# A recurrent chain and a feed-forward layer on one core: four steps of the chain's slot moved, and one more pair of chunks inverted in blocks of 32

## The chip, the cores and the metric

The kernel runs on one core of one Trainium2 chip. A core has TensorE (matrix products and transposes into PSUM), VectorE, ScalarE, GpSimd and a sync engine (SP) that only issues DMAs and waits. Each engine runs its own instructions in order, and the engines meet through semaphores. The metric is the device time of one execution in microseconds; the median of several runs counts. Everything is fp32.

## The reference

For each of 4 batches and 8 heads a state of 40 x 40 is carried over 768 steps; its output, with heads side by side, is the token matrix of a feed-forward layer with a squared relu.

```python
for t in range(S):                                   # S = 768, B = 4, H = 8, D = 40
    y[:, :, t] = einsum('bhd,bhde->bhe', rt, state)
    Sa = einsum('bhde,bhe->bhd', state, at)
    state = state * wt[:, :, None, :] - einsum('bhd,bhe->bhde', Sa, bt)
    state = state + einsum('bhd,bhe->bhde', vt, kt)
x = y.transpose(0, 2, 1, 3).reshape(B * S, H * D)    # 3072 x 320
h = np.maximum(x @ w_in, 0.0)                        # 320 x 2048
out = h * h @ w_out                                  # 2048 x 320
```

## The kernel before

The 768 steps are cut into 6 chunks of 128, and the 4 batches are taken in turn, so that there are 24 chunks: chunk `i` is batch `i % 4`, and a chunk needs the state that chunk `i - 4` left. Inside a chunk the recurrence becomes matrix products: cumulative products of `w` (`decay`, forwards and backwards from the middle of the chunk) scale the inputs, a strictly triangular matrix `N` of products of `b` and `a` has to be inverted, and the rest is products with the state and the masked matrices `A`, `RV` and `RX`.

**Three kinds of work run side by side.**

- *Preparation* (`early`, wrapped by `prepare`): for a chunk some slots ahead, the transposes of `w`, `b`, `a`, the scans (L352, L353) and reciprocals (L357, L358), the products `ps_w<-decay,bT`, and the stores of the decays (`kept_e`) and of `N` (`kept_n`, and by rows `kept_q` or `kept_d`) to DRAM.
- *Inversion on GpSimd* (`take`, `solving`): chunks are grouped in units of 1, 1, 2, 2, 2, 2, 4, 4, 4 and 2. `take` fetches a unit's rows from DRAM into `half_n` (L420) once all its chunks are stored, `solving` runs one multiply and one subtract per step (L448, L450), and L453 stores the result to `kept_t`. The first `FINE` units are inverted in blocks of 32 steps, and their two blocks are then joined by small products on TensorE (`inverses`, second half; it needs the blocks' off-diagonal part, which `early` stores as `kept_m`). The other units are inverted in blocks of 64. The one unit in `AHEAD`, which is `(FINE,)`, is solved in two parts: 33 steps at once, and the rest only after the first part of the next unit's fetch has been issued, in the loop at the end of the kernel. GpSimd waits in order at each fetch for the rows' stores.
- *The chain and the feed-forward layer*: slot `i` runs the eleven pieces of `chain(i)`, and woven between them, for chunk `j = i + 1`: `turn_rv`, `make_rv` (`RV`), `turn_k`, `decay_state`, `turn_down`, `scale_kb`, `turn_state`, `make_a`, and the loading of its inverse (`inverses`, L464 for `T`, L473 for `N`). The layer's work (`Ffn`) is cut into quads (`thirds` and `whole`: the first product, then relu on ScalarE, L735), squares on VectorE (`square`, L742) and quarters (`make_quarter`: the second product and, every fourth time, the output's store).

**What sets the order.** Slots 0 to 3 (`woven`) interleave generators by counts. From slot 4 on `sorted_slot` writes the order out by hand, as a list of `step(...)` calls; after each, `tick` issues the stores that have come due (`later`, `store`; L108). Loads and stores share the sync engine's queue, which works in order; only GpSimd's fetches and result stores go through its own. The buffers concerned: `kept_here` holds the decays (`dec`) of two chunks, the rings of `k`, `b` and `v` two tiles each, the ring of `r` one. At the beginning of slot `i` the local function `loads` issues `k`, `dec` and `b` of chunk `i + 1`. `extra` (only in slot 4) adds quads of the layer, while the weights are still being converted (`rounding`).

Small copies: `turn_k` copies the last decay of the chunk to `ends` (L512), the chain copies its other end to `end` (L664), and `decay_state` multiplies the two (L533) and scales the state in two halves (L536).

Of the kernel before, what the change touches and what calls it, by code (L numbers as in the profile page):

```python
# [11 lines left out]
Alu = mybir.AluOpType  # L12
# [5 lines left out]
def kernel(  # L18
# [22 lines left out]
    nc = tc.nc  # L41
# [4 lines left out]
    C = 128  # L46
# [45 lines left out]
    def new(name, shape, bufs):  # L92
        return work.tile(shape, FP32, tag=name, name=name, bufs=bufs)
# [204 lines left out]
    sizes = [1, 1] + [2] * 4 + [4] * ((len(order) - 12) // 4) + [2]  # L298
    units = [(sum(sizes[:u]), n) for u, n in enumerate(sizes)]

    FINE = 4
    SMALL = units[FINE][0]
    kept_q = dram.tile([SMALL, H, 2, 2, Q, Q], FP32, tag="q", name="kept_q")
    kept_m = [dram.tile([2, Q, H, Q], FP32, tag=f"m{i}", name=f"kept_m{i}") for i in range(SMALL)]
# [120 lines left out]
    def solving(u, between={}, stop=None):  # L425

        first, nb = units[u]
        fine = u < FINE
        size = Q if fine else HC
        cols = classes(u)  # L430
        rows = 128 // cols
        part = part_of(u)
        words = size // cols * size
        at = u * Q * Q // 2 if fine else 0
        ts = solved[:, at:at + words]
        nc.gpsimd.memset(ts, 0.0)
        for col in range(cols):
            nc.gpsimd.memset(ts[col * rows:(col + 1) * rows, col::size + cols], -1.0)
        t3 = ts.rearrange("p (j t) -> p j t", t=size)
        for s in range(size - 1):  # L440
            if s in between:
                between[s]()
            if s == stop:
                yield
            n, m_ = s // cols + 1, size - 1 - s
            at = s * size + s + 1 if s < Q else Q * HC + (s - Q) * (Q + 1) + 1
            p_ = new("half_p", [128, 528], 1)[:, :n * m_].rearrange("p (j t) -> p j t", j=n)
            nc.gpsimd.tensor_tensor(p_, part[:, at:at + m_].unsqueeze(1).to_broadcast([128, n, m_]),  # L448
                                    t3[:, :n, s:s + 1].to_broadcast([128, n, m_]), Alu.mult)
            nc.gpsimd.tensor_tensor(t3[:, :n, s + 1:], t3[:, :n, s + 1:], p_, Alu.subtract)  # L450
        to = kept_t[u]
        to = to.rearrange("n b h f k j t -> (n b h f k) (j t)") if fine else to.rearrange("n b h f j t -> (n b h f) (j t)")
        nc.gpsimd.dma_start(out=to, in_=ts)  # L453
# [53 lines left out]
    def turn_k(i, g):  # L507
        kT, kT_ = turned("kvT", 1), turn(g["x"]["k"])
        down = g["dec"][:, DOWN]
        nc.vector.tensor_tensor(kT, kT_, down[:, :, 1:C + 1], Alu.mult)  # L510
        g["kT"], g["ends"] = kT, new("ends", [128, NP], 2)
        nc.vector.tensor_copy(g["ends"], down[:, :, 0])  # L512

    def make_a(i, g):
        g["A"] = masked("A", 2, g["kT"], g["aT"])
# [11 lines left out]
    def decay_state(i, g):  # L527
        bb, c = order[i]
        if c == 0:
            return  # L530
        st = states.tiles[bb]
        f_ = new("f", [128, NP], 1)
        nc.vector.tensor_tensor(f_, ended[bb], g["ends"], Alu.mult)  # L533
        for e in range(2):
            own_ = st[e * DP:(e + 1) * DP, :, e, :D]
            nc.vector.tensor_tensor(own_, own_, f_[e * DP:(e + 1) * DP].unsqueeze(2).to_broadcast([DP, NP, D]), Alu.mult)  # L536
# [32 lines left out]
    def rest(i, g):  # L569
        begin(i, g)  # L570
        yield
        yield
        turn_k(i, g)
        joining = inverses(i, g) if i else iter(())
        if soon(i):
            next(joining, None)
        yield
        make_a(i, g)
        yield
        turn_rv(i, g)  # L580
        yield
        decay_state(i, g)
        make_rv(i, g)
        if i and unit_of[i] < FINE:
            next(joining)
        yield
        turn_down(i, g)
        yield
        scale_kb(i, g)
        turn_state(i, g)  # L590
        yield
        yield from joining
        yield
# [6 lines left out]
    def chain(i, g):  # L600
# [54 lines left out]
        if c < NCH - 1:  # L655
            grown = psum(ps_c)[:, :NP * 2 * D].rearrange("p (q d) -> p q d", q=NP)
            for l_, r_ in ((k_, v_), (b_, xn)):
                for q in range(NP):
                    mm(grown[:, q].rearrange("p (e d) -> p e d", e=2), pair(l_, q), r_[:, 2 * q:2 * q + 2, :D], l_ is k_ and q == 0)
            for e in range(2):  # L660
                rows = slice(e * DP, (e + 1) * DP)
                nc.vector.tensor_tensor(st[rows, :, e, :D], grown[rows, :, e * D:(e + 1) * D], st[rows, :, e, :D], Alu.add)
            ended[bb] = new(f"end{bb}", [128, NP], 1)
            nc.vector.tensor_copy(ended[bb], g["up"][:, :, C])  # L664
        yield
        rx = masked("RX", 2, xT, rT)
        yield
# [237 lines left out]
    def fetch_next(i, *names):  # L905
        if i < len(order):
            loaded.setdefault(i, {}).update({nm: fetch(nm, {"k": k, "b": b, "r": r, "v": v}[nm], i) for nm in names})

    def sorted_slot(i, g, ch):
        j = i + 1  # L910
        more = j < len(order)
        n = ready.setdefault(j, {}) if more else None
        made = [prepare(m_, apart=True, steps=4 * at) for at, m_ in enumerate(ahead.get(i, ()))]
        one, two = (made + [iter(()), iter(())])[:2]
        joining = inverses(j, n) if more else iter(())
        early_join = more and soon(j)
        fine = more and unit_of[j] < FINE

        def step(*what):
            for w_ in what:  # L920
                w_()
            tick()

        of = lambda fn: (lambda: fn(j, n)) if more else (lambda: None)
        on = lambda gen: lambda: next(gen, None)
        begun = i > B

        def extra():
            if not begun:
                second.thirds()  # L930
                second.whole()

        halves = lambda: [next(rounded, None) for _ in range(2)] if not begun else None

        def loads():
            if more:
                fetch_next(j, "k")
                n["dec"] = kept_here[j % 2]
                nc.sync.dma_start(out=n["dec"][:USED], in_=kept_e[j])
                fetch_next(j, "b")  # L940

        loads()
        step(on(ch), halves)
        if more:
            begin(j, n)
        step(of(turn_rv), on(one), second.make_quarter, on(one), halves)
        step(on(ch), halves)
        if early_join:
            next(joining, None)
        fetch_next(j + 1, "r")  # L950
        step(second.make_quarter, halves)
        extra()
        step(on(ch))
        step(of(make_rv), second.thirds)
        step(on(ch), on(one), on(two), on(two))
        if fine:
            next(joining, None)
        step(second.whole, on(two))
        step(on(ch))
        step(on(one), of(turn_k))  # L960
        step(on(ch), of(decay_state), on(one), of(turn_down), of(scale_kb))
        step(on(ch), of(turn_state), second.square)
        if fine:
            next(joining, None)
        step(on(ch), of(make_a), second.thirds, on(one))
        fetch_next(j + 1, "v")
        step(second.whole, on(two), on(two))
        if not early_join:
            next(joining, None)
        step(on(ch), extra)  # L970
        step(on(ch))
        if more:
            later_chain = n["chain"] = chain(j, n)
            next(later_chain)
        run(ch)
        step(second.square, second.make_quarter)
        step(second.make_quarter, on(two))
        for gen in (one, two, joining):
            run(gen)

    for i in range(len(order)):
        tc.no_sync_barrier()
        g = ready.pop(i)
        ch = first_slot if i == 0 else g["chain"]
        done.update(ahead.get(i, ()))
        if i < B:
            woven(i, g, ch)
            n = ready[i + 1]
            n["chain"] = chain(i + 1, n)
            next(n["chain"])  # L990
            if i == B - 1:
                fetch_next(i + 2, "r", "v")
        else:
            sorted_slot(i, g, ch)
        while unit < len(units) and all(m_ in done for m_ in range(len(order)) if unit_of[m_] == unit):
            flush()
            if under_way:

                take(unit, own, slice(0, EARLIER))
                run(under_way.pop())  # L1000
                take(unit, own, slice(EARLIER, Q * (HC + Q)))
            else:
                take(unit, own)
            if unit in AHEAD:
                under_way.append(solving(unit, stop=Q + 1))
                next(under_way[0])
            else:
                solve(unit)
            unit += 1
# [32 lines left out]
```

## Time and profile before

| what | value |
|---|---|
| runs | 1097.03, 1095.37, 1087.47 us, median 1095.37 |
| profiled execution | 1094.95 us, span 1093.2 us |
| granted TensorE clock, mean | 0.87 |
| TensorE matmuls busy | 952.3 us (87% of the span) |
| TensorE weight loads busy | 785.3 us (72%) |
| GpSimd busy | 669.4 us (61%) |
| VectorE busy | 491.6 us (45%) |
| ScalarE busy | 284.4 us (26%) |
| DMA | 106.92 MB, mean 98 GB/s |
| chain that ended last, by engine | TensorE 66%, VectorE 12%, DMA 8% |

A line of a view names the source line, the engine, the operation and the tiles as `out<-in`; the number in brackets is how long the engine had stood idle before it and who released it. In the table by slices each digit is the busy share of one fortieth of the span (27.3 us) in tenths. The windows' rows give the stretch, its length, the time TensorE was busy and its instructions, the granted clock, the DMA engines' busy share and GB/s. A wait's row gives the waiting engine with its line, who released it, the total, how often and the longest. Matmul ends are modelled, so busy time on TensorE is not work at its peak. L87 is the helper of all plain products and L108 that of delayed stores, so the tiles tell which step a row belongs to.

### The profile page before, as it was taken

The page shows a single profiled execution, that of the slowest core. Times are in us where ns is not written, and L with a number is a line of the kernel's source. Part 1 is how long each engine was busy: PE and PEld are TensorE (multiplying, and loading weights), DVE is VectorE, ACT ScalarE, POOL GpSimd, SP SyncE. Part 2 cuts the span into 40 slices and gives each one's busy share as a digit, 9 for nine tenths or more (in the row PEclk, how much of TensorE's full clock was granted, in tenths as well). Part 3 has the DMA queues.
Part 4 walks back from the last instruction along what each step waited for, and adds up shares of the span by engine and source line. Part 5 has one row for each costly group of instructions (what it writes and reads, how often), then busy time and mean ns, then how long its engine had stood idle before and what let it go on. Part 6 is the DMA issues. An engine that isn't in the chain of part 4 may idle for free.

```text
span 1093.2 us, 19699 instructions
## 1 busy us (share of the span) xinstructions
PE 952.3 (87%) x7728; PEld 785.3 (72%) x7728; DVE 491.6 (45%) x908; ACT 284.4 (26%) x643; POOL 669.4 (61%) x1128
## 2 busy tenths in 40 slices
PE   6275765685899899999899999999999999999998
PEld 5264654674788787778677877878888887777776
DVE  5456683784554435537246345344323433231111
ACT  3133241332231322222312222212222222322111
POOL 4788544886885399993699976999768810000000
PEclk8666575566998898999988998989999999999999
DMA  8878969678144862654873655541644314230000
GB/s 109 145 141 165 174 168 177 147 150 138 43 82 108 143 118 58 98 98 117 142 125 58 100 132 110 95 85 26 136 90 84 65 37 92 47 63 7 13 13 12
DMA packets 261376, 106.92 MB, mean 98 GB/s; under 512 B 244100, under 2 KB 250372, under 8 KB 259620
## 3 DMA queue, kind: packets, MB, share of 16 engines
q1 hardware_dynamic: 256756, 86.65, 44.4%
q0 software_dynamic: 3440, 18.88, 7.5%
q8 instruction: 61, 1.00, 0.4%
q10 hardware_dynamic: 1088, 0.13, 0.1%
q14 instruction: 31, 0.25, 0.1%
HBM read 72.47 MB, written 31.19 MB: 95 GB/s over the span
## 4 chain that ended last, share of the span: by engine, by line
PE 66%; DVE 12%; DMA 8%; issue 4%; ACT 4%; POOL 3%; SPq 2%; ACTq 0%; DVEq 0%; POOLq 0%
PE ps_f L87 36%; PE ps_c L87 13%; PE ps_w L87 11%; PE ps_w L316 4%; DMA in_w<-in_w_dram 2%; DMA dec<-kept_e 2%; DVE hid L742 1%; SPq L108 1%; DVE state L536 1%; PE ps_c L621 1%; POOL half_t L450 1%; POOL half_p L448 1%; DVE RX L332 1%; DMA blocks<-kept_t 1%; DVE kvT L510 1%
## 5 line engine op out<-in xcount | busy, mean ns | idle before, releaser
L448 POOL TENSOR_TENSOR half_p<-half_n,half_t 128x70 f32<-128x70 f32 (+52 forms) x502 | 296.7, 591 | 101.5 <-DMA half_n<-kept_d 51.8
L450 POOL TENSOR_TENSOR half_t<-half_t,half_p 128x70 f32<-128x70 f32 (+52 forms) x502 | 323.4, 644 | 39.3
L87 PE MATMUL ps_f<-w_out,hid 128*128 128x320 f32 x768 | 221.0, 438 | 0.0
L87 PEld LDWEIGHTS ps_f<-w_out,hid 128*128 128x128 f32 x768 | 142.0, 191 | 54.9 <-issue 4.4
L87 PE MATMUL ps_f<-tokens,w_in 128*128 128x256 f32 x672 | 172.7, 415 | 0.0
L87 PEld LDWEIGHTS ps_f<-tokens,w_in 128*128 128x128 f32 x672 | 136.2, 208 | 27.0 <-issue 5.6
L742 DVE TENSOR_TENSOR hid<-hid 128x512 f32<-128x512 f32 x96 | 83.4, 904 | 64.7 <-ACT hid L735 64.7
L332 DVE TENSOR_TENSOR RV<-ps_w,upper 128x512 f32<-128x512 f32 x48 | 30.9, 686 | 154.8 <-PE ps_w L87 154.8
L735 ACT ACTIVATE hid<-ps_f 128x512 f32<-128x512 f32 x84 | 50.2, 597 | 142.5 <-PE ps_f L87 142.5
L683 DVE TENSOR_TENSOR tokens<-ps_c,dec 128x512 f32<-128x512 f32 x24 | 16.6, 690 | 133.5 <-PE ps_c L87 133.5
L87 PE MATMUL ps_w<-decay,bT 40*128 40x128 f32 x352 | 42.1, 373 | 33.2 <-DVE decay L365 22.7
L87 PEld LDWEIGHTS ps_w<-decay,bT 40*128 40x128 f32 x352 | 36.0, 265 | 42.6 <-DVE RX L332 16.2
L87 PE MATMUL ps_f<-tokens,w_third 64*128 64x256 f32 x336 | 54.0, 427 | 6.3 <-DVE w_out L266 6.3
L510 DVE TENSOR_TENSOR kvT<-ps_w,dec 128x512 f32<-128x512 f32 x24 | 16.5, 686 | 86.0 <-ACT minus_x L637 54.1
L372 ACT COPY N<-ps_w 128x512 f32<-128x512 f32 x24 | 14.0, 585 | 147.5 <-PE ps_w L87 114.4
L614 ACT COPY xnT<-ps_c 64x512 f32<-64x512 f32 x24 | 13.9, 579 | 145.7 <-PE ps_c L87 145.6
L352 DVE TENSOR_TENSOR_SCAN decay<-ps_w,ones 128x64 f32<-128x64 f32 x88 | 23.8, 270 | 61.8 <-PE ps_w L316 56.7
L87 PEld LDWEIGHTS ps_f<-tokens,w_third 64*128 64x128 f32 x336 | 37.1, 214 | 9.2 <-DVE w_out L266 6.6
L87 PEld LDWEIGHTS ps_c<-xr,T 64*64 64x64 f32 x768 | 29.4, 146 | 19.6 <-issue 15.6
L87 PE MATMUL ps_w<-dec,kvT 40*128 40x128 f32 x384 | 38.6, 335 | 1.1 <-DVE in_b L551 0.9
L357 DVE RECIPROCAL decay<-decay 128x256 f32<-128x256 f32 x22 | 38.2, 1737 | 0.0
L358 DVE RECIPROCAL decay<-decay 128x256 f32<-128x256 f32 x22 | 37.3, 1696 | 0.0
(137 smaller groups left out, 1479.0 us busy)
## 6 DMA issues: line engine op xcount, KB each, us to landing
kept_e<-decay SPq DMA_DIRECT2D x22, 633.8 KB
dec<-kept_e SPq DMA_DIRECT2D x22, 633.8 KB
hid<-in_moe_w_out_dram SPq DMA_DIRECT2D x16, 320.0 KB
half_n<-kept_d POOLq DMA_DIRECT2D x6, 768.0 KB, 12.1
in_w<-in_w_dram SPq DMA_DIRECT2D x24, 160.0 KB
in_ab<-in_b_dram SPq DMA_DIRECT2D x24, 160.0 KB
in_ab<-in_a_dram SPq DMA_DIRECT2D x24, 160.0 KB
in_k<-in_k_dram SPq DMA_DIRECT2D x24, 160.0 KB
```

Source lines behind the costliest of these rows:

```text
L87: nc.tensor.matmul(o, l_, r_, start=start, stop=True, skip_group_check=True)
L316: nc.tensor.transpose(p_[:, q * 128:(q + 1) * 128], pair(x_, q), ident)
L332: nc.vector.tensor_tensor(t_, p_, over4(upper), Alu.mult)
L352: nc.vector.tensor_tensor_scan(up[:, q, MID + 1:C + 1], wT[:, q, MID:], ones, 1.0, Alu.mult, Alu.mult)
L357: nc.vector.reciprocal(down[:, :, MID + 1:C + 1], up[:, :, MID + 1:C + 1])
L358: nc.vector.reciprocal(up[:, :, :MID], down[:, :, :MID])
L448: nc.gpsimd.tensor_tensor(p_, part[:, at:at + m_].unsqueeze(1).to_broadcast([128, n, m_]), t3[:, :n, s:s + 1].to_broadcast([128, n, m_]), ...
L450: nc.gpsimd.tensor_tensor(t3[:, :n, s + 1:], t3[:, :n, s + 1:], p_, Alu.subtract)
L510: nc.vector.tensor_tensor(kT, kT_, down[:, :, 1:C + 1], Alu.mult)
L683: nc.vector.tensor_tensor(t_, y_, g["up"][:, :, :C], Alu.mult)
L735: nc.scalar.activation(h_, p_.rearrange("p f t -> p (f t)"), Act.Relu)
L742: nc.vector.tensor_tensor(h_, h_, h_, Alu.mult)
```

## The change

Six things are edited. `FINE` goes from 4 to 5, so that unit 4 (chunks 6 and 7) is stored, solved and joined as units 0 to 3 are; the piece of `half_t` that a fine unit uses is taken modulo 4. `decay_state` moves from the chain's sixth piece in the slot to its third, ahead of `make_rv`, and reads the decays' end from `dec` itself, so that `ends` is gone. `turn_state` and the first `square` move behind `make_a`. `extra`'s first call moves behind the chain's fifth piece. The copy of `end` goes from VectorE to ScalarE. `loads` becomes a function of the chunk, puts `dec` first, and is called when a slot's chain has ended, for the chunk after next, in place of the beginning of the next slot; at the end of slot 3, where the loads of chunk 5 are now issued ahead of its `v`, its `r` has been fetched already in the course of that slot.

```diff
-    FINE = 4
+    FINE = 5
...
-        at = u * Q * Q // 2 if fine else 0
+        at = u % 4 * Q * Q // 2 if fine else 0
...
-        g["kT"], g["ends"] = kT, new("ends", [128, NP], 2)
-        nc.vector.tensor_copy(g["ends"], down[:, :, 0])
+        g["kT"] = kT
...
-        nc.vector.tensor_tensor(f_, ended[bb], g["ends"], Alu.mult)
+        nc.vector.tensor_tensor(f_, ended[bb], g["dec"][:, DOWN, :, 0], Alu.mult)
...
         turn_rv(i, g)
+        if i == B:
+            fetch_next(i + 1, "r")
         yield
...
-            nc.vector.tensor_copy(ended[bb], g["up"][:, :, C])
+            nc.scalar.copy(ended[bb], g["up"][:, :, C])
...
+    def loads(j):
+        if j < len(order):
+            n = ready.setdefault(j, {})
+            n["dec"] = kept_here[j % 2]
+            nc.sync.dma_start(out=n["dec"][:USED], in_=kept_e[j])
+            fetch_next(j, "k", "b")
...
-        def loads():
-            if more:
-                fetch_next(j, "k")
-                n["dec"] = kept_here[j % 2]
-                nc.sync.dma_start(out=n["dec"][:USED], in_=kept_e[j])
-                fetch_next(j, "b")
-
-        loads()
         step(on(ch), halves)
...
         step(second.make_quarter, halves)
-        extra()
-        step(on(ch))
+        step(on(ch), of(decay_state))
         step(of(make_rv), second.thirds)
         step(on(ch), on(one), on(two), on(two))
         if fine:
             next(joining, None)
         step(second.whole, on(two))
+        step(on(ch), extra)
+        step(on(one), of(turn_k))
+        step(on(ch), on(one), of(turn_down), of(scale_kb))
         step(on(ch))
-        step(on(one), of(turn_k))
-        step(on(ch), of(decay_state), on(one), of(turn_down), of(scale_kb))
-        step(on(ch), of(turn_state), second.square)
         if fine:
             next(joining, None)
         step(on(ch), of(make_a), second.thirds, on(one))
         fetch_next(j + 1, "v")
-        step(second.whole, on(two), on(two))
+        step(of(turn_state), second.square, second.whole, on(two), on(two))
...
         run(ch)
+        loads(j + 1)
         step(second.square, second.make_quarter)
...
             if i == B - 1:
-                fetch_next(i + 2, "r", "v")
+                loads(i + 2)
+                fetch_next(i + 2, "v")
```

## The prediction

> **What bounds the kernel now.** I read the page's slices first, then the busy time slot by slot, the waits, and last the order of time on GpSimd, VectorE and the sync queue. A slot is one chunk's pass through the chain; I cut at the first copy of `xnT` (L614), whose starts are 249.35 (chunk 4), 311.9, 356.5, 400.6, 442.95, 483.4, 523.9 (chunk 10), 572.0, 613.95, 653.8, 694.65, 736.6 (chunk 15).
>
> ```profile
> PE   6275765685899899999899999999999999999998
> POOL 4788544886885399993699976999768810000000
> PEclk8666575566998898999988998989999999999999
> ```
>
> After the first quarter TensorE has no empty slice, and its clock is not full until about 735 us. Busy TensorE by slot (columns: length, busy, granted clock, DMA share, GB/s):
>
> ```profile
> 356.50:400.60 44.10, 39.61 (x310) 0.85 0.77 143
> ...
> 523.90:572.04 48.14, 41.99 (x309) 0.86 0.73 130
> 572.04:613.95 41.91, 40.05 (x315) 0.88 0.34 58
> ...
> 769.80:802.30 32.50, 32.39 (x286) 1.00 0.82 166
> ```
>
> The last row is a slot that no longer prepares a later chunk: full clock, nothing idle, 32.5 us. The slot of chunk 9 (483.4 to 523.9) runs at clock 1.00 with two preparations in 40.5 us, so a preparation is worth at most 4.0 us, and I take **36.3 us** for a slot with one preparation and nothing in its way. Slots 11 to 14 took 41.9, 39.9, 40.8 and 42.0.
>
> VectorE in slot 11 says where that goes (start, duration, operation):
>
> ```profile
> 587.55 0.65 DVE L512 COPY ends<-dec 128x4 f32<-128x4 f32 x1
> 588.24 0.17 DVE L533 TENSOR_TENSOR f<-end,ends 128x4 f32<-128x4 f32 x1
> 588.44 2.37 DVE L536 TENSOR_TENSOR state<-state,f 64x160 f32<-64x160 f32 x2
> ...
> 593.51 0.85 DVE L664 COPY end<-dec 128x4 f32<-128x4 f32 x1
> 594.28 2.15 DVE L742 TENSOR_TENSOR hid<-hid 128x512 f32<-128x512 f32 x2
> ```
>
> From 587 to 599 it never rests, and TensorE stands still for it twice, 1.49 us for `state` and 0.38 us for `RX`. In sum over the kernel:
>
> ```profile
> DVE kvT L510 <- DMA dec<-kept_e: 24.1, 4, 9.9
> ...
> PE ps_c L561 <- DVE state L536: 11.9, 12, 1.7
> ```
>
> GpSimd is the second path. `L420` fetches a unit's rows, `L453` stores its inverse; the bracket is idle time and its releaser:
>
> ```profile
> 217.85 2.00 POOL L420 DMA_DIRECT2D half_n<-kept_d  x4
> 255.81 0.60 POOL L453 DMA_DIRECT2D kept_t<-half_t  x1 [0.30 <-POOL half_t L450]
> 345.15 0.60 POOL L453 DMA_DIRECT2D kept_t<-half_t  x1 [0.30 <-POOL half_t L450]
> 359.53 1.03 POOL L420 DMA_DIRECT2D half_n<-kept_d  x2 [13.78 <-DMA kept_d<-N]
> 376.48 0.29 POOL L448 TENSOR_TENSOR half_p<-half_n,half_t 128x63 f32<-128x63 f32 x1 [13.70 <-DMA half_n<-kept_d]
> 498.28 0.60 POOL L453 DMA_DIRECT2D kept_t<-half_t  x1 [0.30 <-POOL half_t L450]
> ```
>
> Unit 4 (chunks 6, 7) is stored at 255.8, unit 5 (8, 9) at 345.15, unit 6 (10 to 13) at 498.28. Their first readers on the sync queue come at 311.65, 432.4 and
>
> ```profile
> 519.55 6.53 SPq L464 DMA_DIRECT2D T<-kept_t  x2
> ```
>
> Unit 4 is 50 us early and unit 6 only about 15. The next fault is therefore unit 6.
>
> [...] half-clock stretches of 3.41, 6.83 and 10.24 us, one a slot up to 735.8, though TensorE's idle spells are only 1 to 2 us. [...] one `dec` load takes 6.62 us on the chain at 538.6, but 16.45 us at 359.1, where unit 6's 1.5 MB fetch is issued beside it. [...] the square takes 676 ns at best and 1719 ns at worst.
>
> **The change part by part.** R is the issue of unit 6's fetch, 359.53 before; R' is the same event after.
>
> *Blocks of 32 for unit 4.* Unit 3 has the same shape and took 120.6 to 147.9, 27.3 us; unit 4's two halves took 41.0 (176.88 to 217.85) and 35.7. GpSimd saves some 49 us, hidden on both sides: nobody waited. Added for chunks 6 and 7, each: 32 products of 32x32 (0.5 us per 16 at 283.1 and 310.0), two activations of 0.50, four copies of 0.36 on ScalarE, one 0.43 transpose on VectorE, two stores and two loads of `kept_m` (0.6 to 1.3 us of the sync queue each). In slots 5 and 6 I count 1.5 us of TensorE each; in slot 1 the queue's extra 3 us lie beside a fetch that shrinks from 768 to 512 KB, so 0, between -3 and +4.
>
> *The split solve moves with it.* `AHEAD` is `(FINE,)`, so unit 5 is now the one solved in two parts; in the order of GpSimd's instructions unit 6's fetch stands between the parts. GpSimd is in order. Unit 4 is fetched at 160.7 as now and ends near 198; chunk 9's rows are stored by 209.4, so unit 5's first part, 41 us after a fetch of 14, ends near 267; then GpSimd waits until R' for chunk 13's rows. The second part comes only then: fetch issue 1.0, 35.7, store and rest of the fetch 1.9, wait for the store and clearing 6.9, together 45.5 us before unit 6 starts, where it was 17. It then needs 121.8 (376.48 to 498.28) and 6.8 for the store to land beside the next fetch (as from 646.75 to 653.52 for unit 7): **R'+174**. Unit 5 lands at about R'+44 and is first read near R'+68, covered.
>
> *R'.* Slot 4: the extra quad, which held TensorE for 6.28 us, now follows the first `T` product and 2 us of work slip in ahead of it; the 3.46 us wait for `RX` goes. Slot 5: two preparations of 3.8 on 32.5 and the join, 41.6 against 44.6. The loads now stand ahead of chunk 13's stores: +2.5. Sum -6; I take R' = R-5 (-9 to 0).
>
> *Slots 6 to 9* took 167.4 and would take about 150 (three with one preparation, one with two, one join). None of it is kept: R' lies some 5.5 us into slot 6 and chunk 10's `T` is used 9.5 us into slot 10, so TensorE reaches it at about R'+154 and waits. The queue gets `T(10)` at R'+174; beside unit 7's fetch its two issues take 6.5 as before, `N`, one store and the token moves 8.9, and `dec` of chunk 11 lands 6.6 later: R'+196, with 2.6 for the decay that now stands behind it on VectorE ahead of the `RV` mask: R'+199 = 553. Before, the transpose of `dec` in that slot was at 545.4: **+8** (+2 to +18).
>
> *Decay, squares, copies in slots 10 to 14.* Off the full stretch of VectorE: both copies (0.65+0.85), decay (0.17+2.37, now at a place with 4.9 us idle), squares (2.15, now behind `A`). That is 6.2 us, against stalls of 1.9; the copy on ScalarE is a third of a us in an engine idle three quarters of the time. So the stalls and with them the half-clock stretch go. From slot 10's `dec` transpose to slot 15 took 736.6-545.4 = 191.2. After: 21 for the rest of slot 10, 4x36.3, and 2 for a cold clock after the long wait, 168: **-23** (-10 if the half-clock stretches stay, -26 if the slots are 35.5).
>
> *The loads.* The issues of `dec`, `k`, `b` (1.5 us) go ahead of the stores and the next loads of a finishing slot and behind the token moves. The decay is new in waiting for `dec`, with `RV`, two reciprocals and `kvT` queued behind: landing at about +7 us of a slot against a decay due at +4 costs VectorE 3 us, which fit before `kvT` is due. Taken as 0, up to 3 a slot.
>
> *Slots 15 on* have no stall to lose: 0. Units 7 to 9 run 20 us later than before but their first use has 20 us or more left. Sum: +8-23 = -15 on the profiled execution's 1094.95 (span 1093.2 and 1.75 around it), which is the runs' median 1095.37 but for 0.4: **1080 us**.
>
> **Rivals.** *The clock stays low.* Slots 11 to 14 keep a half-clock stretch because transposes, not stalls, cause it; [...] against it: slot 9 has the same transposes twice and no stretch. Gain -10, sum about -2: **1093**. *Unit 6 later still (slower).* Place: `T(10)`. The same 16.45 us as at 359 for `dec` of chunk 11 (+10), and R' no earlier than R (+5), make +23; with a quarter-warm slot 10 and the low clock the gain is 10: **1108**. It decides from a delay of 23 at that place. *Unit 6 does not hold.* If the second part needed no wait, slots 6 to 10 would be free too: -5-17-12-19, **1042**; against it stands GpSimd's order.
>
> **How the numbers follow.** Forecast 0.52 (1070 to 1088), low clock 0.22 (1088 to 1098), unit 6 later still 0.18 (1098 to 1115), not holding 0.08. The range 1066 to 1104 leaves out the last and a good half of the slower case. One per cent, about what a measurement can tell here since the three runs spread over 0.9, is 1084.4 to 1106.3: faster 0.48, same 0.36, slower 0.16.
>
> **What would show it.** GpSimd idle some 85 us before R', unit 6 stored near 522; TensorE idle 25 to 30 us near 508 to 537; clock 1.00 and 36 to 37 us in slots 11 to 14; no wait of `ps_c` for `state`. Wrong if `T(10)` isn't waited for, or the slots after it keep 40 us.

## The result, and the profile after

The changed kernel takes **1079.34 us**, the median of 20 runs (1073.57 to 1085.31). The kernel before, run beside it, took 1089.92 us, also the median of 20 runs. The measured ratio is 0.9922 (95% interval 0.9897 to 0.9946), 0.8% faster; the quotient of the two medians would be 0.9903. The ratios below are of the same kind, each against the kernel before in the runs of the same session, and 1% of the time of before is about 11 us. The profiled execution took 1076.38 us with a span of 1074.7 us, at a mean granted clock of 0.878.

Line numbers have shifted a little with the change: the chain's first copy is now L615, `decay_state` L532 and L535, `dec`'s transpose L544, the chain's second copy of `minus_x` L638 and the transpose that reads it L651, the square L743. The slots, cut at L615, now start at 248.91 (chunk 4), 311.16, 352.65, 398.88, 433.24, 467.61, 506.05 (chunk 10), 584.81, 619.17, 653.54, 687.91, 722.27 (chunk 15).

The page's slices, TensorE, GpSimd and the granted clock:

```profile
PE   6475766674999699999069999999999999999998
POOL 4788545466000487999769997699976982000000
PEclk9666555666899899999668999999999999999999
```

GpSimd has three slices with nothing in them, 269 to 349 us. TensorE has a slice with almost nothing, the 20th, which was busy before. From the 23rd slice (591 us) on its clock is full to the end, where before slices with a clock of 8 tenths went on up to 738 us.

The windows show the same by slot (length, then busy time on TensorE, its weight loads, VectorE, ScalarE and GpSimd, the clock, the DMA share and GB/s):

```profile
352.65:398.88 46.23, 36.99 (x372) 31.35 (x371) 16.82 (x32) 12.22 (x31) 32.35 (x57) 0.89 0.67 123
398.88:433.24 34.36, 34.36 (x315) 29.28 (x313) 16.83 (x31) 10.09 (x24) 27.19 (x44) 1.00 0.48 104
...
506.05:584.81 78.76, 43.99 (x310) 36.52 (x308) 18.50 (x31) 10.09 (x26) 62.59 (x87) 0.70 0.51 107
584.81:619.17 34.36, 34.36 (x315) 29.29 (x313) 20.06 (x31) 10.09 (x24) 32.22 (x27) 1.00 0.48 76
```

A slot with one preparation is now 34.36 us with TensorE busy for all of it. In slots 7, 8 and 11 to 14 it was 40 to 42 us. Two slots do not fit: slot 6 has 9.2 us with TensorE idle, slot 10 has 34.8.

VectorE in slot 11 shows what has moved (start, duration, operation):

```profile
587.54 0.80 DVE L532 TENSOR_TENSOR f<-end,dec 128x4 f32<-128x4 f32 x1
588.38 1.50 DVE L535 TENSOR_TENSOR state<-state,f 64x160 f32<-64x160 f32 x2
592.49 1.29 DVE L332 TENSOR_TENSOR RV<-ps_w,upper 128x512 f32<-128x512 f32 x2 [2.61 <-PE ps_w L87]
...
604.57 1.28 DVE L332 TENSOR_TENSOR A<-ps_w,upper 128x512 f32<-128x512 f32 x2
605.76 3.15 DVE L743 TENSOR_TENSOR hid<-hid 128x512 f32<-128x512 f32 x2
```

The decay lies ahead of a rest of 2.61 us, and the square, although it took 3.15 us here, has nothing urgent behind it.

GpSimd, at its fetches (L420) and stores (L453), with its idle time in brackets:

```profile
205.00 1.95 POOL L420 DMA_DIRECT2D half_n<-kept_d  x4 [6.60 <-DMA kept_d<-N]
362.26 1.08 POOL L420 DMA_DIRECT2D half_n<-kept_d  x2 [100.53 <-DMA kept_d<-N]
400.78 0.60 POOL L453 DMA_DIRECT2D kept_t<-half_t  x1 [0.30 <-POOL half_t L450]
529.67 0.60 POOL L453 DMA_DIRECT2D kept_t<-half_t  x1 [0.30 <-POOL half_t L450]
```

Unit 5 is fetched at 205.0. Its second part stands behind unit 6's fetch, which waits for the rows of chunk 13, and GpSimd rests with it for 100.5 us. Unit 5 is stored at 400.78 and unit 6 at 529.67. The sync queue and TensorE at the other end of this, slot 10:

```profile
535.02 1.32 SPq L464 DMA_DIRECT2D T<-kept_t  x2
```

```profile
544.50 1.08 PE L87 MATMUL ps_c<-xr,T 64*64 64x40 f32 x16 [33.03 <-DMA tokens<-tokens]
```

The first product with chunk 10's `T` waited 33.03 us. The row names the token moves, which stand next to `T` on the queue; `T` itself could not be issued before 535.02. The sums of waits, to be set against those of before:

```profile
DVE f L532 <- DMA dec<-kept_e: 124.6, 13, 46.4
POOL half_n L420 <- DMA kept_d<-N: 107.1, 2, 100.5
PE ps_c L87 <- DMA tokens<-tokens: 33.0, 1, 33.0
PE ps_c L651 <- ACT minus_x L638: 9.9, 2, 9.2
```

TensorE no longer waits for `state` (11.9 us in 12 waits before), and what it waits for instead is one `T` and, in slot 6, one `minus_x`.

From slot 10's transpose of `dec` on, the account closes: the transpose came at 558.24 instead of 545.38 (+12.9), from there to slot 15 it took 164.0 us instead of 191.2 (-27.2), and from slot 15 to the end 352.4 instead of 356.6 (-4.2). The sum is -18.5 us, which is the difference of the two spans. These are two single executions, and the one before was among its slower ones, the one after among its faster: between the medians of 20 runs the difference is 10.6 us.

### The profile page after: what moved, and what is told of

Its sections match the earlier page's. It is cut to its first block, busy times and chain, and to the rows that moved or that the text cites. A ratio compares the mean times of both kernels' runs of the same rounds, so it can differ in the third digit from the quotient of the medians.

```text
span 1074.7 us, 19908 instructions
## 1 busy us (share of the span) xinstructions
PE 922.2 (86%) x7856; PEld 768.7 (72%) x7856; DVE 480.2 (45%) x866; ACT 289.2 (27%) x675; POOL 622.2 (58%) x1058
## 4 chain that ended last, share of the span: by engine, by line
PE 59%; POOL 18%; DMA 10%; DVE 5%; issue 4%; ACT 3%; SPq 1%; POOLq 0%; DVEq 0%; ACTq 0%
PE ps_f L87 31%; PE ps_c L87 12%; PE ps_w L87 10%; POOL half_t L450 9%; POOL half_p L448 8%; PE ps_w L316 3%; DMA dec<-kept_e 2%; DMA kept_t<-half_t 2%; DMA half_n<-kept_q 1%; PE ps_c L560 1%; PE ps_c L651 1%; DMA kept_e<-decay 1%; DMA T<-kept_t 1%; DMA in_v<-in_v_dram 1%; DMA blocks<-kept_t 1%
## 5 line engine op out<-in xcount | busy, mean ns | idle before, releaser
L448 POOL TENSOR_TENSOR half_p<-half_n,half_t 128x70 f32<-128x70 f32 (+50 forms) x470 | 276.0, 587 | 87.7 <-DMA half_n<-kept_d 31.6
L450 POOL TENSOR_TENSOR half_t<-half_t,half_p 128x70 f32<-128x70 f32 (+50 forms) x470 | 299.4, 637 | 36.8
L87 PE MATMUL ps_f<-tokens,w_in 128*128 128x256 f32 x672 | 159.7, 392 | 0.0
L87 PEld LDWEIGHTS ps_f<-tokens,w_in 128*128 128x128 f32 x672 | 128.4, 196 | 18.7 <-issue 1.0
L743 DVE TENSOR_TENSOR hid<-hid 128x512 f32<-128x512 f32 x96 | 86.2, 935 | 49.7 <-ACT hid L736 49.7
L420 POOL DMA_DIRECT2D half_n<-kept_d x16 | 8.1, 509 | 107.7 <-DMA kept_d<-N 107.1
L87 PE MATMUL ps_c<-xr,T 64*64 64x40 f32 x768 | 36.1, 243 | 35.4 <-DMA tokens<-tokens 33.0
L532 DVE TENSOR_TENSOR f<-end,dec 128x4 f32<-128x4 f32 x20 | 6.6, 329 | 124.6 <-DMA dec<-kept_e 124.6
L87 PE MATMUL ps_w<-decay,bT 40*128 40x128 f32 x352 | 33.1, 335 | 23.8 <-DVE decay L365 21.9
L615 ACT COPY xnT<-ps_c 64x512 f32<-64x512 f32 x24 | 13.9, 578 | 137.6 <-PE ps_c L87 137.5
L87 PEld LDWEIGHTS ps_w<-decay,bT 40*128 40x128 f32 x352 | 30.6, 240 | 27.4 <-issue 15.4
L332 DVE TENSOR_TENSOR RX<-ps_w,upper 128x512 f32<-128x512 f32 x48 | 30.9, 686 | 28.2 <-PE ps_w L87 28.1
```

The lines of the kernel that those rows point to most:

```text
L87: nc.tensor.matmul(o, l_, r_, start=start, stop=True, skip_group_check=True)
L332: nc.vector.tensor_tensor(t_, p_, over4(upper), Alu.mult)
L615: nc.scalar.copy(xc[low], xw[low])
L743: nc.vector.tensor_tensor(h_, h_, h_, Alu.mult)
```

## Experiments: the blocks of 32 and the divided solve

**The changed kernel without the division.**

```diff
-    AHEAD, under_way = (FINE,), []
+    AHEAD, under_way = (), []
```

> The changed kernel with no unit solved in two parts. Theory (GpSimd's split of unit 5 makes chunk 10's inverse late and swallows what slots 6 to 9 gain): unit 6 starts 17 us after its fetch instead of 46, is stored near 501 instead of 530, the 33 us wait of TensorE for chunk 10 goes, slots 11 to 14 stay at 34.4, and the time falls by some 30 us against the changed kernel, to about 1048. Rival (the wait of chunk 10 stands for something else, such as the token moves or the loads in the sync queue): the wait stays above 20 us and the time stays at 1075 to 1082.

Measured: 1050.34 us, ratio 0.9619 (0.9576 to 0.9661). The wait for chunk 10's `T` fell from 33.03 to 1.03 us, and unit 6 was stored at 497.64. So the division moved to unit 5 costs the changed kernel some 30 us: 29 by the medians, 3.0% of the time of before by the ratios.

**The moves alone**, with unit 4 in blocks of 64 and itself the one that is divided, as before.

```diff
-    FINE = 5
+    FINE = 4
```

> The changed kernel with unit 4 back in blocks of 64 (it is then again the one solved in two parts): only the moves of decay, squares, copies and loads are left. Theory: unit 6 stored near 503, chunk 10 waits 0 to 8 us, no join in slots 5 and 6, so that slot 6 loses its 9 us stall: about 1042, ahead of the kernel without the split by a few us; blocks of 32 for chunks 6 and 7 bring nothing. Rival (the shorter inversion is what gave the gain): 1085 to 1095, as the kernel before.

Measured: **1042.13 us**, ratio 0.9539 (0.9490 to 0.9588). Both halves of the change taken together give 0.8%; the moves by themselves give 4.6%. Slot 10 is better but not free. It takes 56.2 us at a granted clock of 0.79, where it took 78.8 in the changed kernel:

```profile
508.74 1.08 PE L87 MATMUL ps_c<-xr,T 64*64 64x40 f32 x16 [13.68 <-DMA tokens<-tokens]
```

With slots of 34 us TensorE is at chunk 10 early. GpSimd fetched unit 6 at 359.11, after a rest of 14.3 us for chunk 13's rows, and stored it at 494.33: even without a divided solve in between, this fetch and solve are the bound there.

**The blocks alone**: the kernel before with `FINE = 5` and the offset modulo 4, with the division (first), and without it (second, with the edit of `AHEAD` shown above added).

```diff
-    FINE = 4
+    FINE = 5
...
-        at = u * Q * Q // 2 if fine else 0
+        at = u % 4 * Q * Q // 2 if fine else 0
```

> The kernel before with unit 4 in blocks of 32 and nothing else (unit 5 is then the one in two parts). Theory: unit 6 29 us later, chunk 10 reached at about the same time as before, so that 8 to 15 us are lost: about 1101 against 1090. Rival (the shorter inversion gains by itself): 1075 to 1085.

> The kernel before with unit 4 in blocks of 32 and no unit in two parts. Theory: unit 6 as early as before, the joins of chunks 6 and 7 cost 3 to 6 us of slots 5 and 6: about 1094. Rival (GpSimd's saving of 50 us is worth time): 1080 or less.

Measured: 1100.20 us, ratio 1.0078 (1.0049 to 1.0106), and 1103.85 us, ratio 1.0108 (1.0063 to 1.0153). The first came out at the expected figure, but not for the expected reason: its slot 10 waits only 1.8 us for what stands with `T`, and what it lost is in slot 6, which took 52.1 us instead of 44.1. In the old order, with slots of some 40 us, the late unit 6 is still nearly in time, so the division costs nothing there; without it the kernel is not faster. That second kernel missed its figure by 10 us, and its loss is in slot 6 too (56.0 us). The waits of each in slot 6, first with and then without the division:

```profile
PE ps_c L650 <- ACT minus_x L637: 10.9, 1, 10.9
```

```profile
PE ps_c L650 <- ACT minus_x L637: 15.0, 1, 15.0
```

In the changed kernel the same wait is 9.24 us. The rows ahead of it, on ScalarE, VectorE and the sync queue of the changed kernel:

```profile
373.49 0.91 ACT L484 ACTIVATE T<-blocks,which 128x256 f32<-128x256 f32 x2 [11.71 <-DMA blocks<-kept_t]
```

```profile
373.50 0.45 DVE L482 STREAM_TRANSPOSE spares<-blocks 128x256 f32<-128x256 f32 x1 [8.98 <-DMA blocks<-kept_t]
```

```profile
364.05 4.75 SPq L470 DMA_DIRECT2D blocks<-kept_t  x2
```

The join of chunk 7 reads `blocks`, whose load is issued at 364.05, 1.8 us after unit 6's 1.5 MB fetch. Both engines stand at their first instruction of the join until it lands, and behind it on ScalarE stand the copies of `minus_x` that the chain needs next. The reading is that not the join's work but its place in two in-order engines makes the price.

**The same load earlier.** To test this reading, the kernel without the division issues what the join of chunk 7 reads at the end of slot 5, ahead of `dec`; TensorE's, VectorE's and ScalarE's orders stay.

```diff
-    AHEAD, under_way = (FINE,), []
+    AHEAD, under_way = (), []
...
-        joining = inverses(j, n) if more else iter(())
+        joining = (n.pop("join", None) or inverses(j, n)) if more else iter(())
...
-        if early_join:
+        if early_join and j != 7:
             next(joining, None)
...
         run(ch)
+        if j == 6:
+            n7 = ready.setdefault(7, {})
+            n7["join"] = inverses(7, n7)
+            next(n7["join"])
         loads(j + 1)
```

> The changed kernel without the divided solve (as in the run that left the division out), and the loads that the join of chunk 7 needs are issued at the end of slot 5, ahead of dec, k and b of chunk 7. Theory (the join costs 9 to 15 us in slot 6 because its load stands beside unit 6's fetch and ScalarE and VectorE wait for it in order): the wait of ps_c for minus_x in slot 6 falls from 11.8 to below 3 us and slot 6 from 52 to some 41; the end hardly moves, since chunk 10's T is then waited for by about the same time: 1046 to 1052. Rival (the join's own work on VectorE and ScalarE costs it): slot 6 stays at 50 or more.

Measured: 1048.16 us, ratio 0.9594 (0.9527 to 0.9661). Slot 6 without and with the edit:

```profile
353.60:406.00 52.40, 40.57 (x373) 34.61 (x372) 18.38 (x32) 12.27 (x31) 30.23 (x43) 0.80 0.64 119
```

```profile
350.50:386.20 35.70, 35.70 (x372) 30.18 (x371) 16.23 (x32) 12.38 (x31) 10.65 (x21) 1.00 0.91 171
```

The slot loses 16.7 us and TensorE does not rest in it, with the same instructions on it but for one record. And the end does not move beyond its interval (0.9619 without the edit). A row of that kernel in slot 10 shows why:

```profile
514.10 1.08 PE L87 MATMUL ps_c<-xr,T 64*64 64x40 f32 x16 [15.33 <-DMA T<-kept_t]
```

The time won is spent waiting for unit 6. In the changed kernel, too, the stall of slot 6 lies behind unit 6's fetch and in front of the 33 us wait, so that by the same reasoning it costs nothing at the end; no run took it out of that kernel itself.

## Experiments: what the moves are made of

All of these start from the moves alone (1042.13, ratio 0.9539) and take something back.

**All that concerns VectorE**: decay, squares with `turn_state`, and both small copies at their old places (the copies' edit is shown further below, and the decay reads `ends` again). Loads and `extra` stay moved.

```diff
-        step(on(ch), of(decay_state))
+        step(on(ch))
...
-        step(on(ch), on(one), of(turn_down), of(scale_kb))
-        step(on(ch))
+        step(on(ch), of(decay_state), on(one), of(turn_down), of(scale_kb))
+        step(on(ch), of(turn_state), second.square)
...
-        step(of(turn_state), second.square, second.whole, on(two), on(two))
+        step(second.whole, on(two), on(two))
```

> Blocks of 64 for unit 4, the loads and the extra quad as changed, but decay_state, the squares with turn_state, and both small copies all back at their old places on VectorE. Theory (VectorE's relief is the whole gain of the moves, and its parts cover for each other: undone one at a time they gave back 11, 15 and 2 of 50 us): slots 11 to 14 return to 40 to 42 us with a half-clock stretch each, no wait of note for chunk 10's T, about 1092 to 1100. Rival (the parts simply add up): 28 us more than 1042, about 1070. Rival (the loads carry a part): 1080 or less, with slots 11 to 14 below 39.

Measured: 1083.63 us, ratio 0.9925 (0.9890 to 0.9961). Against 0.9539 that is 3.9% of the time of before, some 42 us: the theory had VectorE's part as the whole gain, and it is most of it but not all. What is left, the moved loads and `extra`, is worth 0.8% (0.4 to 1.1) under the old order. Slots 11 and 14 of it:

```profile
559.60:599.80 40.20, 38.36 (x315) 32.15 (x313) 21.16 (x33) 10.13 (x24) 37.69 (x33) 0.92 0.39 64
...
674.00:716.10 42.10, 40.30 (x314) 33.42 (x313) 20.72 (x33) 10.15 (x24) 39.28 (x37) 0.88 0.47 91
```

TensorE waits for `state` and `RX` again, 3.6 and 3.9 us between 540 and 720, and its clock is below full in these two slots. Slots 12 and 13, which were to be at 40 us or more too, took 38.0 and 36.2.

**One part at a time.** The decay, still reading `dec`:

```diff
-        step(on(ch), of(decay_state))
+        step(on(ch))
...
-        step(on(ch), on(one), of(turn_down), of(scale_kb))
+        step(on(ch), of(decay_state), on(one), of(turn_down), of(scale_kb))
```

> Blocks of 64 for unit 4 and all the moves but one: decay_state stands again at its old step, with the transpose of dec, behind kvT on VectorE. Theory (the gain comes from TensorE's stalls in slots 4 to 14 and the half-clock stretch that each brings; one stall is enough for a stretch): the wait of ps_c for state returns at 1 to 1.7 us a slot and with it most half-clock stretches, so about 5 of the 6.5 us a slot that slots 7 to 14 lost: about 1077. Rival (the gain is shared out by VectorE's time, 2.5 of 6.2 us): about 1061. Rival (the loads carry it): 1042 to 1046.

The squares:

```diff
-        step(on(ch))
+        step(on(ch), of(turn_state), second.square)
...
-        step(of(turn_state), second.square, second.whole, on(two), on(two))
+        step(second.whole, on(two), on(two))
```

> Blocks of 64 for unit 4 and all the moves but one: the squares, with turn_state, stand again ahead of the A mask. Theory (stalls and the stretch each brings): RX and A come some 2.2 us later on VectorE; RX had 0.4 us to spare with the decay gone, so TensorE waits 1 to 2 us for RX again in slots 6 to 14 and part of the half-clock stretches return: about 1060, the point at which one stall decides being unknown (1050 to 1075). Rival (shared out by VectorE's time, 2.2 of 6.2 us): about 1058, but with the clock still full in slots 11 to 14. Rival (the loads carry it): 1042 to 1046.

The copies (`ends` is copied, and nothing reads it):

```diff
-        g["kT"] = kT
+        g["kT"], g["ends"] = kT, new("ends", [128, NP], 2)
+        nc.vector.tensor_copy(g["ends"], down[:, :, 0])
...
-            nc.scalar.copy(ended[bb], g["up"][:, :, C])
+            nc.vector.tensor_copy(ended[bb], g["up"][:, :, C])
```

> Blocks of 64 for unit 4 and all the moves but one: end is copied on VectorE again and ends is copied again behind kvT (nothing reads it now, it only takes its time). Theory: 0.5 to 0.85 us each on VectorE, of which RX's mask is 1 to 1.5 us later with 0.4 to spare: a stall of up to 1 us a slot, mostly too short for a stretch: about 1048. Rival (shared out by VectorE's time, 1.5 of 6.2 us): about 1054. Rival (the loads carry it): 1042.

Measured: decay back 1053.22 us, ratio 0.9643 (0.9568 to 0.9719); squares back 1057.05, ratio 0.9651 (0.9591 to 0.9711); copies back 1043.89, ratio 0.9537 (0.9480 to 0.9595). The decay's theory foresaw 1077 and is wrong: no wait of TensorE for `state` comes back. Single steps give back 1.0, 1.1 and 0.0% of the time of before, in sum 2.1, where all three together give back 3.9. By the ratios alone this is only just clear of noise, as the decay's four runs lie between 1046 and 1061 and its interval touches that of the moves alone. The traces say the same more plainly: slots 11 to 14 take 140.8 us together in the moves alone, 143.7, 144.6 and 141.2 with one part back, and 156.5 with all three. That is 7.1 us one by one and 15.7 together. The parts cover for each other. The likely reason, not shown apart, is that VectorE's stretch from `kvT` to `A` has room for one of them and not for both. A rival that shares out the gain by VectorE's time (2.5, 2.2 and 1.5 of 6.2 us) would have the copies give back 1%, which their interval leaves hardly any room for.

**The loads at the beginning of the slot again**, and `r` and `v` of chunk 5 at the end of slot 3 as before (the local `loads` of before is back as well).

```diff
...
+        loads()
         step(on(ch), halves)
...
         run(ch)
-        loads(j + 1)
...
-                loads(i + 2)
-                fetch_next(i + 2, "v")
+                fetch_next(i + 2, "r", "v")
```

> Blocks of 64 for unit 4 and all the moves but one: k, dec and b are issued again at the start of the slot that uses them, and r and v of chunk 5 in slot 3. Theory: dec then lands 5 to 8 us into the slot where the decay stands at 4, so VectorE waits up to 4 us with RV and the reciprocals behind it; kvT has 1 to 3 us to spare, so TensorE loses 1 to 3 us a slot in some slots and part of the clock; chunk 4's v is no longer behind two loads: about 1055. Rival (the loads carry the gain): 1075 or more. Rival (dec still comes in time): 1040.

Measured: **1036.38 us**, ratio 0.9460 (0.9403 to 0.9517), the lowest ratio of all. The decay does wait for `dec` (119.8 us in 14 waits), but slots 7 to 14 other than 10 stay at 34.4 us (38.4 in slot 9, with two preparations), so moving the loads bought nothing there once the rest was moved. Slot 4 took 56.3 us instead of 62.2. A row of slot 4 in the changed kernel suggests why:

```profile
260.39 1.09 PE L316 MATMUL ps_w<-ident,in_v 128*128 128x128 f32 x4 [10.66 <-DMA in_v<-in_v_dram]
```

**`v` ahead of the moved loads** at the end of slot 3, to see whether this order alone does it.

```diff
-                loads(i + 2)
                 fetch_next(i + 2, "v")
+                loads(i + 2)
```

> The moves with blocks of 64 for unit 4, but v of chunk 5 is fetched ahead of dec, k and b of chunk 5 at the end of slot 3. Theory (slot 4 lost its 6 us because its v stood behind three loads on the sync queue): the 10.17 us wait for in_v in slot 4 falls to 4 or 5, slot 4 takes 56 to 57 us instead of 62.2, unit 6 is fetched 4 to 6 us earlier, and what follows is as it was: about 1037. Rival ([...] the order on the queue does not matter): slot 4 stays at 62, 1042.

Measured: 1035.91 us, ratio 0.9487 (0.9421 to 0.9552). The wait for `in_v` in slot 4 fell from 10.2 to 3.7 us and the slot to 55.5 us. Its ratio cannot be told from that of the kernel with the old loads.

## An experiment that failed: unit 6 earlier still

The kernel with the old loads still waits 9.48 us for chunk 10's `T`. Here the fetch of each unit of four chunks is issued in two parts, the first three chunks' rows as soon as GpSimd is free.

```diff
+        later_rows = nb == 4
         for col in range(cols):
-            queues[col % len(queues)].dma_start(out=part_of(u)[col * rows:(col + 1) * rows, words], in_=kept[:, words])
+            own_ = slice(0, rows - rows // nb) if later_rows else slice(0, rows)
+            queues[col % len(queues)].dma_start(out=part_of(u)[col * rows + own_.start:col * rows + own_.stop, words], in_=kept[own_, words])
+        if later_rows:
+            for col in range(cols):
+                queues[0].dma_start(out=part_of(u)[(col + 1) * rows - rows // nb:(col + 1) * rows, words], in_=kept[rows - rows // nb:, words])
```

> The moves but for the loads (1036 before), and each fetch of a unit of four chunks is issued in two parts: the rows of its first three chunks, which are long stored, as soon as GpSimd is free, and those of the fourth when they land. Theory (chunk 10's T is waited for some 12 us, and unit 6's fetch is what starts it): GpSimd begins unit 6 about 4 us earlier than 367, the wait for T of chunk 10 falls by as much: about 1032. Rival (the last rows' fetch takes as long as the whole[...]): no earlier start, 1036.

Measured: 1044.91 us, ratio 0.9581 (0.9502 to 0.9660), 8 us above the kernel that it edits, though the intervals of the ratios touch. The first step came, in part, as expected: GpSimd's first product on unit 6 stands at 360.73, 6.3 us earlier than the 367.02 of the kernel it edits. But slot 6 itself began 3.3 us earlier in this execution, so 3.0 us are the edit's, where 4 were expected. GpSimd, with the fetch in two parts:

```profile
344.36 1.02 POOL L422 DMA_DIRECT2D half_n<-kept_d  x2
347.20 0.99 POOL L425 DMA_DIRECT2D half_n<-kept_d  x2 [1.82 <-DMA kept_d<-N]
360.73 0.29 POOL L453 TENSOR_TENSOR half_p<-half_n,half_t 128x63 f32<-128x63 f32 x1 [9.35 <-DMA half_n<-kept_d]
```

Then the same slot on the sync queue, VectorE and TensorE:

```profile
346.45 4.75 SPq L943 DMA_DIRECT2D dec<-kept_e  x1
```

```profile
363.85 0.25 DVE L537 TENSOR_TENSOR f<-end,dec 128x4 f32<-128x4 f32 x1 [20.01 <-DMA dec<-kept_e]
```

```profile
365.77 1.11 PE L316 MATMUL ps_w<-ident,in_k 128*128 128x128 f32 x4 [10.36 <-DVE RV L332]
```

The chain of waits gives the load's whole time:

```profile
346.45 17.38 DMA dec<-kept_e
```

Chunk 7's `dec` is now issued behind the fetch instead of ahead of it, and takes 17.4 us beside it. In the kernel it edits, the decay started at 358.02, 13.1 us into slot 6; here it is 22.3 us into it. Since the decay was moved ahead of `RV`, a late `dec` holds VectorE with `RV` behind it, and TensorE waits 10.36 us for that. Slot 6 becomes 46.8 us instead of 37.4. In slot 10 the wait for `T` is gone, but waits of 6.75 us for `in_w` and 6.09 us for `RV` stand there instead, and the slot takes 54.2 us instead of 54.8.

## Why the prediction was right

Forecast 1080, measured 1079.34. The mechanism that was forecast is the one that was found: the divided solve holds unit 6, TensorE waits for chunk 10's `T`, and what VectorE's relief wins is won behind that wait. That the two figures agree to within 1 us is luck. The forecast took 15 us off a median of 1095.37 from three runs, and over 20 runs the one before took 1089.92, so that the medians are only 10.6 us apart. And by step, several errors cancel:

- *Blocks of 32 for unit 4, 49 us on GpSimd hidden.* Right. They ended in a rest of 100.5 us (85 foreseen).
- *The division moves and holds unit 6: `R'`+174.* Right: `T` could be issued at 535.02, `R'`+172.8, and the wait for it was 33 us where 25 to 30 were foreseen. Taking the division away removed it.
- *`R'` = `R`-5, at most `R`.* **Wrong**: 362.26, `R`+2.7. Of the -6 that the prediction sums, slot 5 was to give 3 and gave 3.1, so slot 4 was to give some 5.5; it gave 0.3. Its waits for `RX` (3.5 us) and `in_r` (4.6) did go, but `v` was put behind three loads and was waited for 10.66 us; with `v` first the slot is 55.5. And the loads ahead of chunk 13's stores were put at 2.5 us, but the fetch came 9.6 us into slot 6 instead of 3.0, which is 6.6. The loads' place alone is worth 4.3 of this: in the moves alone the fetch comes 10.4 us into the slot, with the loads at their old place 6.1.
- *Slot 5 41.6, slots 6 to 9 about 150.* Measured 41.5 and 153.4, for two errors that met: slots with one preparation were 34.4 and not 36.3, and slot 6 had the 9.24 us of the join, which was counted at 1.5. The step that failed there is the counting of the join by its instructions alone; that its first instructions wait for a load, in order ahead of the chain's copies, was not priced. It did not show in the end, as slots 6 to 9 were rightly held to be absorbed by the wait.
- *Slot 10's transpose of `dec` +8.* Measured +12.9: `R'` was 7.7 us later than taken, and the rest of the way from `R'` was 196.0 and not 199.
- *The decay, the squares, the copies: -23 to slot 15.* Measured -27.2. The four slots at 34.4 instead of 36.3 are 7.7 us shorter than foreseen, since a slot with one preparation takes 1.9 us more than one without, and not 3.8. The rest of slot 10, put at 23, of which 2 were the author's estimate for a lower clock after the wait, took 26.6, as before the change, each time with 10.24 us at half clock in it (563.77 to 574.01; before, 551.22 to 561.46), and lost 3.6 of that again. The clock is full (1.00) in slots 11 to 14 with the same transposes as before, so the rival in which transposes hold the clock down is out. That the relief of VectorE is the cause is shown by taking it back from the moves alone (1083.63).
- *Slots 15 on: 0.* Measured -4.2. Slot 15 went from 33.2 us to 32.5 and slots 20 to 22 from 31.7 to 31.1 each; the waits for `state` there, four of 0.7 us at most, had been put at nothing and are gone. The rest was not taken apart.

So +8-23+0 = -15 became +12.9-27.2-4.2 = -18.5. The rival in which unit 6 does not hold was put at 1042; without the division it is 1050.34, and 1042.13 in the moves alone. In the trace without the division and with the join's loads moved ahead, unit 6 is fetched 5.5 us and stored 5.3 us later than in the moves alone, which is most of the difference; the rest was not taken apart. "Unit 6 later still" named the right place but needed a delay of 23, and it was 12.9.

One thing the prediction left open is which stall lowers the clock. Slot 10, with the 33 us wait, has a mean clock of 0.70, and its record shows half clock from 515.98 to 553.53. The prediction's reading of the records, one half-clock stretch a slot, was not exact: before the change slot 9 has no such stretch, slot 10 has two, one of 13.65 us stands in slot 6, and the last of that row ends at 725.3, not at 735.8. Nor does the amount of idle time in a slot decide. The kernel with VectorE's parts back has slots of 38.0 and 36.2 us (599.8 to 674.0) at clock 1.00 with TensorE idle for 2.2 and 0.9 us in them, and slots 11 and 14 at 0.92 and 0.88 with 1.8 us idle each.

The traces before and after the change show it more closely. In both the clock's record changes only at multiples of 3.41 us from its first entry, so each trace can be cut into stretches of that length. From 280 us on there are 423 whole ones at full clock, and 16 of them are followed by half clock. Of the 391 with TensorE idle for less than 0.40 us none is followed by it, of the 5 with 1.8 us or more all are, and of the 27 in between 11 are; what decides there was not shown. (The ends of matmuls are modelled, so the idle times are those of the modelled record.) In 17 of the 423 transposes took over 1.5 us and other products under 1.6, and half clock followed none of them.

## What to carry to other kernels

When a helper engine works through a queue of jobs in order, a change that makes one job cheaper can make the next one late: look for what waits *between* the jobs, and read the deadline of the job after. Price an instruction that waits for a transfer by what stands behind it in its engine and by what large transfer lies beside it, not by its own duration (the join was counted at 1.5 us and cost TensorE a wait of 9.24); moving it earlier makes it stricter about its data (the moved decay waited 20.01 us for a late `dec`). And test the halves of a double change apart: here one half was worth some 50 us and the other took about 40 of them.

## What was not expected of the hardware

- That a load of `dec` takes far longer beside the 1.5 MB fetch was seen before the change (16.45 us against 6.62). Not expected was how much 2 us of order do. Issued 0.4 us ahead of the fetch, before the change, it took 16.45 us. In the kernel with the old loads, issued at 349.03, 2.0 us ahead of the fetch at 351.02, it took 9.0 and had landed by 358.0. In the kernel with the fetch in two parts, issued at 346.45, 2.1 us behind the fetch at 344.36, it took 17.4. In the changed kernel, 9.2 us ahead, it took 6.0. In these traces, one of each kind, a head start of 2 us takes away most of the delay.
- Two relief measures on VectorE, each worth about 1% when taken back alone (for one of them hardly clear of noise), are worth 3.9% together with the third one, which alone was worth nothing. TensorE's stalls did not add up here by the time removed: slots 11 to 14 lose 2.9, 3.8 and 0.4 us with one part back and 15.7 with all three.
